# Narrowing the gated layer's weights in 54 smaller steps, at other places of the expert loop

## The chip, the cores and the metric

One core of one Trainium2 chip runs the whole program. The metric is the device time of one execution in microseconds (us), the lower the better. Engines are called TensorE (PE in the profile, its weight loads PEld), VectorE (DVE), ScalarE (ACT), GpSimd (POOL) and SyncE (SP, which only issues transfers here).

## What is computed

Three layers follow one another on 3072 tokens of width 384. The weights of all three come in as 64-bit floats.

```
attention: state = f * state + k v^T;  y = q state        (4 x 8 heads, 768 steps, width 48)
x = y as [3072, 384]
experts:   logits = x @ w_gate; each token goes to one of 8 experts, 384 tokens each, by falling logit
           out[tokens of e] = relu(x @ w1[e]) @ w2[e]     (w1[e]: 384 x 1024, w2[e]: 1024 x 384)
gated:     xn = x / rms(x) * rms_g
           result = (silu(xn @ w_gate) * (xn @ w_val)) @ w_out     (384 x 1536, 384 x 1536, 1536 x 384)
```

## The kernel before

**The stages.** The program runs attention and the routing of the tokens to experts (to about 150 us), the eight experts one after the other (to about 372 us), and the gated layer in twelve chunks of 256 tokens (to the end).

**Matrix products.** Each product of 32-bit floats is made of three matmuls (`mm3`, L620 to L624): both operands are split into a high part and a remainder, and high x high, remainder x high and high x remainder are added up in PSUM. So each operand needs a rounding on ScalarE (the high part) and a subtraction, on VectorE as a rule (the remainder).

**An expert** (`expert`, L1068) is a loop over j = 0 to 7, called slots here. In slot j TensorE makes `h` of block j of 128 hidden columns (nine matmuls of 384 columns), ScalarE takes the relu and rounds it (`hh`, L1082), VectorE makes its remainder (`hl`, L1083), and TensorE multiplies block j - 2 by its piece of w2 (`second`, L979, nine matmuls into `x2`). After slot 7 the `second` of blocks 6 and 7 follow at once, and ScalarE copies `x2` out (`finish`, L975). Each engine works through its instructions in the order of the program.

**Beside it** `side` (L1035) puts in each slot the work for later: in slots 1 to 4 one of the four weight pieces of the next expert is split (`piece_split`, L806: `w`, 1536 columns, ScalarE and then VectorE L813); slots 5 to 7 turn and split the next expert's tokens (`xpose`, L962: three transposes into `xT`, then `xhi` on ScalarE and `xlo` on VectorE L973); slot 0 gathers the tokens of the expert after (`gather`, three indirect transfers on GpSimd); `w_load` issues the loads of pieces on SyncE's queue (L803). In the last expert the pieces of the gated layer take their place (`w2_load`, `piece_split(W2[...])`, two of them on GpSimd).

**Narrowing.** The gated layer's weights are too large to be used as 64-bit floats, and are turned to 32 bits while the experts run, written to DRAM (`w32`) and read from there by `w2_load`. A call of `narrow_step` (L1016) does up to three things, each for another step: it issues the store of a finished step on ScalarE's queue (L1018), works on a step whose load was issued two calls before (`narrow2`, L998), and issues the load of a new one on SyncE's queue (`narrow`, L995). `narrow2` is one multiplication on ScalarE (`nr`, L1004), three integer operations on VectorE (`nb` L1005, `nb` L1006, `ne` L1008) and two on GpSimd (a multiplication L1009 and an addition L1010). A step is 128 x 384 weights; there are 36 of them, and an expert has a call in each of slots 1 to 4, 6 and 7. The first two slots of an expert without a call are 0 and 5.

**The last expert.** In its slot 0 the squares of the first chunk of the gated layer are added up (`n0.squares`, L905: squares on ScalarE, `ss` L911 and the remainder `sl` L915 on VectorE; they lie in `nraw` buffers), and in its slot 2, behind `second`, TensorE sums them over the partitions (`n0.total`, L919 and L920).

**What sets the order** around the change is the program's text alone: `side` is called at the end of a slot's code, and every engine and queue takes its part of it in that order. Buffers of a name rotate; a tile's next use waits for the last reader of its former content.

Of the kernel before, what the change touches and what calls it, by code (L numbers as in the profile page):

```python
# [7 lines left out]
F32 = mybir.dt.float32  # L8
F32R = mybir.dt.float32r
BF = mybir.dt.bfloat16  # L10
I32 = mybir.dt.int32
# [69 lines left out]
class Route:  # L81
# [27 lines left out]
    def range(self, n):  # L109

        nc, v = self.tc.nc, self.v
        m = self.m0[:, 0:n]
        nc.vector.tensor_reduce(out=m, in_=self.lg[:, 0:n], axis=AX.X, op=OP.max)
        nc.vector.tensor_reduce(out=v[:, 1:2], in_=self.lg[:, 0:n].rearrange("p n e -> p (n e)"), axis=AX.X, op=OP.min)
        nc.vector.tensor_reduce(out=v[:, 0:1], in_=m, axis=AX.X, op=OP.max)
        nc.vector.tensor_reduce(out=v[:, 2:3], in_=m, axis=AX.X, op=OP.min)
        nc.vector.tensor_scalar(v[:, 1:3], v[:, 1:3], -1.0, None, op0=OP.mult)
        self.n = n
# [623 lines left out]
def tile_kernel(ctx, tc, q, k, v, f_logit, w_gate, w1, w2, w2_gate, w2_val, w2_out, rms_g, fT, kT, qT, vL, out):  # L742
# [11 lines left out]
    wide = w2_gate.dtype != F32  # L754
# [43 lines left out]
    def piece(pool, rpool, src, shape, eng, hold=False):  # L798

        raw = rpool.tile([128, 1536], F32, name="wraw").rearrange("p (a b) -> p a b", a=shape[0])  # L800
        if hold:
            nc.gpsimd.memset(raw[0:1, 0, 0:1], 0.0)
        nc.sync.dma_start(raw, src)  # L803
        return [pool, raw, shape, eng]

    def piece_split(p, cp=None):  # L806
        pool, raw, shape, eng = p
        hi, lo = (pool.tile([128, 1536], F32R, name="w").rearrange("p (a b) -> p a b", a=shape[0]) for _ in range(2))
        if cp is None:
            nc.scalar.copy(hi, raw)  # L810
        else:
            cp.tensor_scalar(hi, raw, 1.0, 0.0, op0=OP.mult, op1=OP.add)
        eng.tensor_tensor(out=lo, in0=raw, in1=hi.bitcast(F32), op=OP.subtract)  # L813
        p[:] = [(hi, lo)]
# [8 lines left out]
    def w_src(e, i):  # L823
        s = slice((i % 2) * 512, (i % 2) * 512 + 512)
        if i < 2:
            return w1[e, :, s].rearrange("(c p) f -> p c f", p=128), (KD, 512)
        return w2[e, s].rearrange("(c p) f -> p c f", p=128), (4, DM)
# [4 lines left out]
    def gather(e):  # L832
        if e not in XG:
            XG[e] = [xp.tile([128, DM], F32, name="xrow") for _ in range(KD)]
        for c, t in enumerate(XG[e]):
            nc.gpsimd.indirect_dma_start(out=t, out_offset=None, in_=x_dram[:, :],
                                         in_offset=bass.IndirectOffsetOnAxis(
                                             ap=idx[:, 3 * e + c:3 * e + c + 1], axis=0))
# [3 lines left out]
    def w_load(e, i):  # L842
        W1[e, i] = piece(wpool, rawp, *w_src(e, i), nc.vector, e == 1 and i < 2)
# [10 lines left out]
    with ExitStack() as st:  # L854
        with tc.tile_pool(name="rw", bufs=9) as rw, tc.tile_pool(name="rwp", bufs=4, space=PSUM) as rwp:
            rows = Rows(tc, YT, x_dram, ident, rw, rwp)
            rows.put(2)
            rows.take(2)
            R = R[0]
            R.copy()  # L860
            w_load(0, 0)

            def side(s):
                if s < 3:
                    w_load(0, s + 1)
                if 0 < s < 5:
                    pool, raw, shape, _ = W1[0, s - 1]
                    hi, lo = (pool.tile([128, 1536], F32R, name="w").rearrange("p (a b) -> p a b", a=shape[0])
                              for _ in range(2))
                    nc.scalar.copy(hi, raw)  # L870
                    parts[s - 1] = hi, lo, raw

            R.run(5, flag, idx, ident, rows, side)
            gather(0)
# [65 lines left out]
    def prep(c, d, X, eng):  # L940
        s = xn[:, d, c * TC:(c + 1) * TC]
        hi, lo = (t[:, d, 0:TC] for t in X)
        nc.scalar.copy(hi, s)  # L943
        eng.tensor_tensor(out=lo, in0=s, in1=hi.bitcast(F32), op=OP.subtract)  # L944

    W2 = {}
    with ExitStack() as c1:
        P = lambda name, bufs, **kw: c1.enter_context(tc.tile_pool(name=name, bufs=bufs, **kw))
        hp = P("m1h", 3, side="right")
        tp = P("m1t", 1, side="right")  # L950
# [5 lines left out]
        def w2_load(i):  # L956
            if i < 7:
                W2[i] = piece(wpool, rawp, *w2_src(i), nc.gpsimd if i in (1, 3) else nc.vector)
# [3 lines left out]
        def xpose(e, d):  # L962
            if d == 0:
                XT[e] = xt_tiles()
            o = psT.tile([128, CAP], F32, name="xT")
            for c in range(3):
                nc.tensor.transpose(o[:, c * 128:(c + 1) * 128], XG[e][c][:, d * 128:(d + 1) * 128], ident)
            split(e, d, o)
# [13 lines left out]
                mm3(nc, x2[m], [t[:, j % 4, m * 128:(m + 1) * 128] for t in w], H[j], j == 0, j == KF - 1)  # L982

        def nraw():
            return tp.tile([128, 384, 2], I32, name="nraw", bufs=3)

        def narrow(i, h):

            n = 384
            src = w64[i].rearrange("a b -> (a b)").rearrange("(h p c) -> h p c", p=128, c=2 * n)[h]  # L990
            dst = w32[i][:, :].rearrange("a b -> (a b)").rearrange("(h p c) -> h p c", p=128, c=n)[h]
            raw = nraw()
            if len(todo) > 33:
                nc.gpsimd.memset(raw[0:1, 0:1], 0)
            nc.sync.dma_start(raw.rearrange("p c two -> p (c two)"), src)  # L995
            return raw, dst

        def narrow2(raw, dst):  # L998
            n = 384
            hw, lw = raw[:, :, 1], raw[:, :, 0].bitcast(U32)  # L1000
            b = tp.tile([128, n], I32, name="nb", bufs=2)
            e2 = tp.tile([128, n], I32, name="ne")
            r = tp.tile([128, n], F32, name="nr", bufs=3)
            nc.scalar.mul(r, lw, 2.0 ** -52)  # L1004
            nc.vector.tensor_scalar(b, hw, 3, 0x3FFFFFFF, op0=OP.logical_shift_left, op1=OP.bitwise_and)  # L1005
            nc.vector.scalar_tensor_tensor(out=b, in0=hw, scalar=-0x40000000, in1=b, op0=OP.bitwise_and,  # L1006
                                           op1=OP.bitwise_or)
            nc.vector.tensor_scalar(e2, b, -0x800000, None, op0=OP.bitwise_and)  # L1008
            nc.gpsimd.tensor_tensor(out=r, in0=r, in1=e2.bitcast(F32), op=OP.mult)  # L1009
            nc.gpsimd.tensor_tensor(out=r, in0=r, in1=b.bitcast(F32), op=OP.add)  # L1010
            return dst, r

        todo = [(i, h) for i in range(3) for h in range(12)] if wide else []
        ready, done = [], []

        def narrow_step():  # L1016
            if len(done) > 1 or (done and not ready):
                nc.scalar.dma_start(*done.pop(0))  # L1018
            if len(ready) > 1 or (ready and not todo):
                done.append(narrow2(*ready.pop(0)))  # L1020
            if todo:
                ready.append(narrow(*todo.pop(0)))
# [3 lines left out]
        def first_parts():  # L1026
            X0.extend(xt_tiles())
            return [t[:, 0, 0:TC] for t in X0]

        n0 = Norm(0, tp, psT, "xT", lambda n: nraw().rearrange("p c two -> p (c two)").bitcast(F32)[:, :TC], first_parts)  # L1030
        tail0 = n0.steps()[2:]
        NORM0 = {(E - 1, 0): [n0.squares], (E - 1, 2): [n0.total], (E - 1, 3): tail0[0:2], (E - 1, 4): tail0[2:3]}
        del tail0[:3]

        def side(e, j):  # L1035
            if e + 1 < E:
                if j == 0:
                    gather(e + 1)
                    w_load(e + 1, 1)
                if 0 < j < 5:  # L1040
                    narrow_step()
                    piece_split(W1[e + 1, j - 1])
                if j in (1, 2):
                    w_load(e + 1, j + 1)
                if j > 4:
                    xpose(e + 1, j - 5)
                if j == 7:
                    if e + 2 < E:
                        w_load(e + 2, 0)
                    else:  # L1050
                        w2_load(0)
                if j > 5:
                    narrow_step()
            else:
                if j < 6:
                    w2_load(j + 1)
                if j:
                    piece_split(W2[j - 1])
                if j == 5:
                    for f in tail0:  # L1060
                        f()
                if j == 6:
                    for d in range(KD):
                        prep(0, d, X0, nc.gpsimd)
            for f in NORM0.get((e, j), ()):
                f()
# [60 lines left out]
    with ExitStack() as c1:  # L1127
# [35 lines left out]
        for c in range(NCH):  # L1163
            O = [psO.tile([128, DM], F32, name=f"o{m}") for m in range(MB)]
            Hs = {}
            for j in range(KG):
# [10 lines left out]
                h = hp.tile([128, T], F32, name="hf")  # L1177
# [76 lines left out]
```

## Time and profile before

| | |
|---|---|
| time, median of three runs | 832.44 us (831.95 to 832.62) |
| profiled execution | 832.29 us |
| its span, first to last instruction | 830.6 us |
| TensorE: matmuls busy | 805.3 us, 97% of the span |
| TensorE: weight loads busy | 777.4 us, 94% |
| VectorE, ScalarE, GpSimd busy | 485.7, 391.3, 274.0 us |
| mean granted clock of TensorE | 0.985 of full speed; 1.00 in the experts |

The span is the time from the first to the last instruction in the trace; the execution's own time is 1.69 us longer, by what lies around it. Busy matmuls overlap, so that a busy TensorE is not one at its peak. The views read below are the page's busy times, the waits by engine, busy times by stretch, and timelines: a row of a timeline has the start in us from the start of the span, the length, the engine, the line, the operation with its output and inputs, and in brackets how long the engine was idle before it and what ended that. A group of three matmuls may be printed as one row (x3).

### The profile page before, as it was taken

The page shows a single profiled execution, that of the slowest core. Times are in us where ns is not written, and L with a number is a line of the kernel's source. Part 1 is how long each engine was busy: PE and PEld are TensorE (multiplying, and loading weights), DVE is VectorE, ACT ScalarE, POOL GpSimd, SP SyncE. Part 2 cuts the span into 40 slices and gives each one's busy share as a digit, 9 for nine tenths or more (in the row PEclk, how much of TensorE's full clock was granted, in tenths as well). Part 3 has the DMA queues.
Part 4 walks back from the last instruction along what each step waited for, and adds up shares of the span by engine and source line. Part 5 has one row for each costly group of instructions (what it writes and reads, how often), then busy time and mean ns, then how long its engine had stood idle before and what let it go on. Part 6 is the DMA issues. An engine that isn't in the chain of part 4 may idle for free.

```text
span 830.6 us, 16688 instructions
## 1 busy us (share of the span) xinstructions
PE 805.3 (97%) x6641; PEld 777.4 (94%) x6641; DVE 485.7 (58%) x875; ACT 391.3 (47%) x834; POOL 274.0 (33%) x327
## 2 busy tenths in 40 slices
PE   8999996999999999999999999999999999999996
PEld 7888875899999999999999999999999999999996
DVE  8988868579888988575444434334343434334332
ACT  5777644256645555476343343424343443434221
POOL 7877600367777777250202010110102010110100
PEclk9999997899999999999999999999999999999999
DMA  9997227586887788341000000000000000000000
GB/s 270 224 219 193 58 92 290 184 298 226 284 280 245 248 282 301 127 152 39 10 12 20 1 20 2 20 1 20 4 17 20 1 21 1 20 1 21 1 20 20
DMA packets 43829, 88.56 MB, mean 107 GB/s; under 512 B 5440, under 2 KB 23104, under 8 KB 43744
## 3 DMA queue, kind: packets, MB, share of 16 engines
q1 hardware_dynamic: 34672, 70.89, 27.6%
q0 software_dynamic: 3072, 9.44, 3.4%
q10 hardware_dynamic: 6000, 7.09, 2.4%
q8 instruction: 54, 0.88, 0.5%
q14 instruction: 31, 0.25, 0.1%
HBM read 70.89 MB, written 16.52 MB: 105 GB/s over the span
## 4 chain that ended last, share of the span: by engine, by line
PE 61%; issue 9%; DVE 8%; ACT 2%; DMA 1%; POOL 1%; ACTq 0%; DVEq 0%; POOLq 0%
PE o L624 5%; PE o L622 5%; PE o L623 5%; PE g L622 5%; PE g L624 5%; PE g L623 5%; PE v L624 5%; PE v L623 5%; PE v L622 5%; PE x L623 3%; PE x L624 2%; PE x L622 2%; DVE nb L1006 2%; DVE w L813 2%; PE h L623 2%
## 5 line engine op out<-in xcount | busy, mean ns | idle before, releaser
L1178 DVE TENSOR_TENSOR hf<-sg,v 128x256 f32<-128x256 f32 x144 | 60.0, 417 | 165.1 <-PE v L624 114.9
L944 POOL TENSOR_TENSOR xlo<-xn,xhi 128x256 fp32r<-128x256 f32 x36 | 29.5, 823 | 311.9 <-ACT xhi L943 311.9
L1181 ACT CAST hh<-hf 128x256 fp32r<-128x256 f32 x144 | 58.6, 407 | 132.9 <-DVE hf L1178 132.9
L624 PE MATMUL g<-xhi,w 128*128 128x256 f32 x432 | 119.3, 276 | 0.0
L623 PE MATMUL g<-xlo,w 128*128 128x256 f32 x432 | 119.3, 276 | 0.0
L624 PE MATMUL v<-xhi,w 128*128 128x256 f32 x432 | 119.2, 276 | 0.0
L622 PE MATMUL v<-xhi,w 128*128 128x256 f32 x432 | 119.2, 276 | 0.0
L623 PE MATMUL v<-xlo,w 128*128 128x256 f32 x432 | 119.2, 276 | 0.0
L622 PE MATMUL g<-xhi,w 128*128 128x256 f32 x432 | 119.2, 276 | 0.0
L1182 DVE TENSOR_TENSOR hl<-hf,hh 128x256 fp32r<-128x256 f32 x144 | 61.3, 426 | 68.1 <-ACT hh L1181 67.6
L624 PE MATMUL o<-w,hl 128*128 128x384 f32 x288 | 98.6, 342 | 0.0
L622 PE MATMUL o<-w,hh 128*128 128x384 f32 x288 | 97.5, 339 | 0.2 <-ACT hh L1181 0.2
L623 PE MATMUL o<-w,hh 128*128 128x384 f32 x288 | 97.1, 337 | 0.0
L1176 ACT ACTIVATE sg<-g 128x256 f32<-128x256 f32 x144 | 55.3, 384 | 87.8 <-PE g L624 87.3
L622 PEld LDWEIGHTS g<-xhi,w 128*128 128x128 f32 x432 | 81.1, 188 | 0.0
L624 PEld LDWEIGHTS g<-xhi,w 128*128 128x128 f32 x432 | 81.1, 188 | 0.0
L622 PEld LDWEIGHTS v<-xhi,w 128*128 128x128 f32 x432 | 81.1, 188 | 0.0
L624 PEld LDWEIGHTS v<-xhi,w 128*128 128x128 f32 x432 | 81.1, 188 | 0.0
L623 PEld LDWEIGHTS v<-xlo,w 128*128 128x128 f32 x432 | 81.1, 188 | 0.0
L623 PEld LDWEIGHTS g<-xlo,w 128*128 128x128 f32 x432 | 81.0, 188 | 0.0
L1009 POOL TENSOR_TENSOR nr<-nr,ne 128x384 f32<-128x384 f32 x36 | 61.6, 1711 | 42.8 <-ACT hh L1082 11.8
L623 PE MATMUL x<-hl,w 128*128 128x384 f32 x192 | 65.7, 342 | 3.5 <-DVE hl L1083 3.5
(237 smaller groups left out, 1893.8 us busy)
## 6 DMA issues: line engine op xcount, KB each, us to landing
wraw<-in_moe_w_dram SPq DMA_DIRECT2D x32, 768.0 KB, 7.8
v<-in_v_rows_dram SPq DMA_DIRECT2D x16, 288.0 KB, 5.1
x_dram<-xrows SPq DMA_DIRECT2D x24, 192.0 KB, 5.4
nraw<-in_moe_w_gate_dram SPq DMA_DIRECT2D x12, 384.0 KB, 4.9
nraw<-in_moe_w_val_dram SPq DMA_DIRECT2D x12, 384.0 KB, 4.4
nraw<-in_moe_w_out_dram SPq DMA_DIRECT2D x12, 384.0 KB, 4.3
raw_f<-in_f_logit_turned_dram SPq DMA_DIRECT2D x26, 144.0 KB, 5.4
raw_k<-in_k_turned_dram SPq DMA_DIRECT2D x26, 144.0 KB, 4.6
```

The costliest lines, as they stand in the source:

```text
L622: nc.tensor.matmul(out, lhs[0], rhs[0], start=first, stop=False)
L623: nc.tensor.matmul(out, lhs[0], rhs[1], start=False, stop=False)
L624: nc.tensor.matmul(out, lhs[1], rhs[0], start=False, stop=last)
L813: eng.tensor_tensor(out=lo, in0=raw, in1=hi.bitcast(F32), op=OP.subtract)
L944: eng.tensor_tensor(out=lo, in0=s, in1=hi.bitcast(F32), op=OP.subtract)
L1006: nc.vector.scalar_tensor_tensor(out=b, in0=hw, scalar=-0x40000000, in1=b, op0=OP.bitwise_and, op1=OP.bitwise_or)
L1009: nc.gpsimd.tensor_tensor(out=r, in0=r, in1=e2.bitcast(F32), op=OP.mult)
L1176: nc.scalar.activation(sg, pg, AF.Silu)
L1178: nc.vector.tensor_tensor(out=h, in0=sg, in1=pv, op=OP.mult)
L1181: nc.scalar.copy(hh, h)
L1182: nc.vector.tensor_tensor(out=hl, in0=h, in1=hh.bitcast(F32), op=OP.subtract)
```

## The change

A step becomes 128 x 256 weights, so that there are 54. Calls of `narrow_step` are taken out of slots 1 to 4. Slots 5, 6 and 7 of each expert but the last now have two calls, and so has slot 0 of experts 1 to 6; in the last expert slots 0, 1 and 2 have two each, in which the last two steps are worked on and the last stores issued. A step waits one call longer for its store. The buffers are more and smaller: `nraw` four, `nb` three, `ne` two and `nr` five in place of three, two, one and three, which is 18,432 bytes of a partition before and after. Before the first four loads (three before) GpSimd touches the buffer.

```diff
--- before.py
+++ after.py
@@ -982,25 +982,25 @@
                 mm3(nc, x2[m], [t[:, j % 4, m * 128:(m + 1) * 128] for t in w], H[j], j == 0, j == KF - 1)
 
         def nraw():
-            return tp.tile([128, 384, 2], I32, name="nraw", bufs=3)
+            return tp.tile([128, 256, 2], I32, name="nraw", bufs=4)
 
         def narrow(i, h):
 
-            n = 384
+            n = 256
             src = w64[i].rearrange("a b -> (a b)").rearrange("(h p c) -> h p c", p=128, c=2 * n)[h]
             dst = w32[i][:, :].rearrange("a b -> (a b)").rearrange("(h p c) -> h p c", p=128, c=n)[h]
             raw = nraw()
-            if len(todo) > 33:
+            if len(todo) > 49:
                 nc.gpsimd.memset(raw[0:1, 0:1], 0)
             nc.sync.dma_start(raw.rearrange("p c two -> p (c two)"), src)
             return raw, dst
 
         def narrow2(raw, dst):
-            n = 384
+            n = 256
             hw, lw = raw[:, :, 1], raw[:, :, 0].bitcast(U32)
-            b = tp.tile([128, n], I32, name="nb", bufs=2)
-            e2 = tp.tile([128, n], I32, name="ne")
-            r = tp.tile([128, n], F32, name="nr", bufs=3)
+            b = tp.tile([128, n], I32, name="nb", bufs=3)
+            e2 = tp.tile([128, n], I32, name="ne", bufs=2)
+            r = tp.tile([128, n], F32, name="nr", bufs=5)
             nc.scalar.mul(r, lw, 2.0 ** -52)
             nc.vector.tensor_scalar(b, hw, 3, 0x3FFFFFFF, op0=OP.logical_shift_left, op1=OP.bitwise_and)
             nc.vector.scalar_tensor_tensor(out=b, in0=hw, scalar=-0x40000000, in1=b, op0=OP.bitwise_and,
@@ -1010,11 +1010,11 @@
             nc.gpsimd.tensor_tensor(out=r, in0=r, in1=b.bitcast(F32), op=OP.add)
             return dst, r
 
-        todo = [(i, h) for i in range(3) for h in range(12)] if wide else []
+        todo = [(i, h) for i in range(3) for h in range(18)] if wide else []
         ready, done = [], []
 
         def narrow_step():
-            if len(done) > 1 or (done and not ready):
+            if len(done) > 2 or (done and not ready):
                 nc.scalar.dma_start(*done.pop(0))
             if len(ready) > 1 or (ready and not todo):
                 done.append(narrow2(*ready.pop(0)))
@@ -1037,8 +1037,10 @@
                 if j == 0:
                     gather(e + 1)
                     w_load(e + 1, 1)
+                if e and not j:
+                    narrow_step()
+                    narrow_step()
                 if 0 < j < 5:
-                    narrow_step()
                     piece_split(W1[e + 1, j - 1])
                 if j in (1, 2):
                     w_load(e + 1, j + 1)
@@ -1049,9 +1051,13 @@
                         w_load(e + 2, 0)
                     else:
                         w2_load(0)
-                if j > 5:
+                if j > 4:
+                    narrow_step()
                     narrow_step()
             else:
+                if j < 3:
+                    narrow_step()
+                    narrow_step()
                 if j < 6:
                     w2_load(j + 1)
                 if j:
```

VectorE in an expert of the middle, before: slots 0 and 1 (the two `hl` at the top) and the start of slot 2. The names are those above; `x2` merges two like rows.

```order
L1083 SCALAR_TENSOR_TENSOR hl<-h,hh 128x384 x2
L1005 TENSOR_SCALAR nb<-nraw 128x384
L1006 SCALAR_TENSOR_TENSOR nb<-nraw,nb 128x384
L1008 TENSOR_SCALAR ne<-nb 128x384
L813 TENSOR_TENSOR w<-wraw,w 128x1536
L1083 SCALAR_TENSOR_TENSOR hl<-h,hh 128x384
L1005 TENSOR_SCALAR nb<-nraw 128x384
```

Slot 1 is a step and a piece, and slots 2 to 4 repeat it. Slots 5 to 7, before:

```order
L1083 SCALAR_TENSOR_TENSOR hl<-h,hh 128x384
L973 TENSOR_TENSOR xlo<-xT,xhi 128x384
L1083 SCALAR_TENSOR_TENSOR hl<-h,hh 128x384
L973 TENSOR_TENSOR xlo<-xT,xhi 128x384
L1005 TENSOR_SCALAR nb<-nraw 128x384
L1006 SCALAR_TENSOR_TENSOR nb<-nraw,nb 128x384
L1008 TENSOR_SCALAR ne<-nb 128x384
L1083 SCALAR_TENSOR_TENSOR hl<-h,hh 128x384
L973 TENSOR_TENSOR xlo<-xT,xhi 128x384
```

Here slot 5 has no step, and slots 6 and 7 have one each. VectorE at the end of slot 4, in slots 5 and 6 and at the start of slot 7 with the change (lines of `expert` are six higher there):

```order
L813 TENSOR_TENSOR w<-wraw,w 128x1536
L1089 SCALAR_TENSOR_TENSOR hl<-h,hh 128x384
L973 TENSOR_TENSOR xlo<-xT,xhi 128x384
L1005 TENSOR_SCALAR nb<-nraw 128x256
L1006 SCALAR_TENSOR_TENSOR nb<-nraw,nb 128x256
L1008 TENSOR_SCALAR ne<-nb 128x256
L1005 TENSOR_SCALAR nb<-nraw 128x256
L1006 SCALAR_TENSOR_TENSOR nb<-nraw,nb 128x256
L1008 TENSOR_SCALAR ne<-nb 128x256
L1089 SCALAR_TENSOR_TENSOR hl<-h,hh 128x384
L973 TENSOR_TENSOR xlo<-xT,xhi 128x384
L1005 TENSOR_SCALAR nb<-nraw 128x256
L1006 SCALAR_TENSOR_TENSOR nb<-nraw,nb 128x256
```

Between two `hl` of slots 1 to 4 there was a step and a piece, and is now a piece alone; between the `hl` of slots 5, 6 and 7 and the one behind each there were no, one and one step, and are now two.

VectorE in slot 0 of the last expert, with the change; before, the rows from L1005 to L1008 were not there:

```order
L1089 SCALAR_TENSOR_TENSOR hl<-h,hh 128x384
L1005 TENSOR_SCALAR nb<-nraw 128x256
L1006 SCALAR_TENSOR_TENSOR nb<-nraw,nb 128x256
L1008 TENSOR_SCALAR ne<-nb 128x256
L1005 TENSOR_SCALAR nb<-nraw 128x256
L1006 SCALAR_TENSOR_TENSOR nb<-nraw,nb 128x256
L1008 TENSOR_SCALAR ne<-nb 128x256
L911 TENSOR_TENSOR nraw<-nraw 128x256 x2
L915 TENSOR_TENSOR xlo<-nraw,xhi 128x256
```

The two steps stand ahead of the squares that `n0.total` sums.

## Rows read from the trace of the kernel before

**Rows 1.** One expert each: length, then PE, PEld, DVE, ACT, POOL busy us, clock, DMA.

```profile
233.85:261.48 27.63, 26.87 (x155) 26.16 (x153) 24.27 (x34) 14.77 (x24) 20.91 (x15) 1.00 0.80 264
316.69:343.11 26.42, 26.42 (x154) 26.31 (x153) 20.62 (x28) 13.40 (x21) 15.46 (x11) 1.00 0.85 295
```

**Rows 2.** Waits, weight loads of TensorE (whole span): total us, times, longest.

```profile
PEld x L623 <- DVE hl L1083: 6.2, 9, 1.1
```

**Rows 3.** Timeline of one expert, weight loads of TensorE: start, us, [idle before].

```profile
255.47 0.19 PEld L623 LDWEIGHTS x<-hl,w 128*128 128x128 f32 x1 [0.29 <-DVE hl L1083]
259.98 0.19 PEld L623 LDWEIGHTS x<-hl,w 128*128 128x128 f32 x1 [1.07 <-DVE hl L1083]
```

**Rows 4.** The same expert, VectorE: `hl` of slot 5, then slots 6 and 7.

```profile
259.37 0.55 DVE L1083 SCALAR_TENSOR_TENSOR hl<-h,hh 128x384 fp32r<-128x384 f32 x1
261.23 0.39 DVE L1005 TENSOR_SCALAR nb<-nraw 128x384 int32<-128x384 int32 x1
261.66 0.56 DVE L1006 SCALAR_TENSOR_TENSOR nb<-nraw,nb 128x384 int32<-128x384 int32 x1
262.32 0.36 DVE L1008 TENSOR_SCALAR ne<-nb 128x384 int32<-128x384 int32 x1
262.60 0.55 DVE L1083 SCALAR_TENSOR_TENSOR hl<-h,hh 128x384 fp32r<-128x384 f32 x1
263.53 0.52 DVE L1005 TENSOR_SCALAR nb<-nraw 128x384 int32<-128x384 int32 x1
264.08 1.26 DVE L1006 SCALAR_TENSOR_TENSOR nb<-nraw,nb 128x384 int32<-128x384 int32 x1
```

**Rows 5.** The same expert, GpSimd beside them.

```profile
260.39 1.02 POOL L1010 TENSOR_TENSOR nr<-nr,nb 128x384 f32<-128x384 f32 x1
262.82 1.01 POOL L1009 TENSOR_TENSOR nr<-nr,ne 128x384 f32<-128x384 f32 x1 [1.41 <-ACT xhi L972]
263.91 1.02 POOL L1010 TENSOR_TENSOR nr<-nr,nb 128x384 f32<-128x384 f32 x1
```

**Rows 6.** GpSimd and VectorE in expert 1, slot 1.

```profile
188.70 1.02 POOL L1009 TENSOR_TENSOR nr<-nr,ne 128x384 f32<-128x384 f32 x1 [0.37 <-issue]
189.79 2.42 POOL L1010 TENSOR_TENSOR nr<-nr,nb 128x384 f32<-128x384 f32 x1
...
188.82 2.51 DVE L813 TENSOR_TENSOR w<-wraw,w 128x1536 fp32r<-128x1536 f32 x1 [0.26 <-issue]
```

**Rows 7.** Operations of 256 columns: GpSimd (min/median/max ns), VectorE (page, mean ns).

```profile
L944 POOL TENSOR_TENSOR xlo<-xn,xhi x36: 733/737/2288, 366.6 to 782.2; 128x256 fp32r<-128x256 f32 x36
...
L1182 DVE TENSOR_TENSOR hl<-hf,hh 128x256 fp32r<-128x256 f32 x144 | 61.3, 426 | 68.1 <-ACT hh L1181 67.6
```

**Rows 8.** Timeline of expert 6, where TensorE waits for nothing.

```profile
336.10 0.49 PE L967 MATMUL xT<-ident,xrow 128*128 128x128 f32 x3
343.11 0.49 PE L967 MATMUL xT<-ident,xrow 128*128 128x128 f32 x3
345.21 0.34 PE L623 MATMUL x<-hl,w 128*128 128x384 f32 x1
...
344.15 0.56 DVE L973 TENSOR_TENSOR xlo<-xT,xhi 128x384 fp32r<-128x384 f32 x1 [1.34 <-ACT xhi L972]
```

**Rows 9.** Expert 7: VectorE in slot 0, TensorE at the end of slot 2.

```profile
348.93 0.56 DVE L1083 SCALAR_TENSOR_TENSOR hl<-h,hh 128x384 fp32r<-128x384 f32 x1 [4.23 <-ACT hh L1082]
349.54 0.95 DVE L911 TENSOR_TENSOR nraw<-nraw 128x256 f32<-128x256 f32 x2
350.97 0.42 DVE L915 TENSOR_TENSOR xlo<-nraw,xhi 128x256 fp32r<-128x256 f32 x1 [0.47 <-ACT xhi L914]
...
353.10 0.28 PE L920 MATMUL xT<-xlo,onesr 128*128 128x256 f32 x1
```

**Rows 10.** The page, DMA issues: KB each, median us to landing.

```profile
wraw<-in_moe_w_dram SPq DMA_DIRECT2D x32, 768.0 KB, 7.8
nraw<-in_moe_w_gate_dram SPq DMA_DIRECT2D x12, 384.0 KB, 4.9
```

## The prediction

> **What bounds the kernel now.** TensorE, nearly everywhere: its matmuls are busy for 97% of the span (the table). So the change can give back only what TensorE waits for in the experts, where the steps are, or add to it. I read the waits of TensorE's weight loads first: those for `hl` are 6.2 us in nine times [rows 2], and no other wait of theirs falls in the experts' loop. Then two stretches, each from the last transposes of one expert to those of the next: 27.63 us where there are such waits, with the matmuls busy for 26.87; 26.42 us, all busy, where there are none [rows 1]. In the first a short and a long wait (0.29 and 1.07 us, in slots 6 and 7) cost 1.21 [rows 1, 3], so about 0.08 less than each lasts. Nine waits then cost 6.2 - 9 x 0.08 = **5.5 us**: experts 1 to 5, in each the long one, in four the short one too. Expert 6, which has only two steps left, has none.
>
> The timeline of VectorE tells why. In slots 1 to 4 it has a step, a piece and `hl`, more than a slot of TensorE lasts (about 3.2 us, 3.5 with transposes: the transposes of slots 5 and 7 are 7.01 us apart [rows 8]). So `hl` of slot 5 ends at 259.92 [rows 4], and the weight load that waits for it starts at 259.98 [rows 3].
>
> **Two rules read from the rows.** (1) VectorE's operations on SBUF and GpSimd's exclude each other. Alone, a step runs 261.23 to 262.60, 1.37 us; the next one's first `nb` ends 0.22 after GpSimd's multiplication, its second (1.26 for 0.56) 0.41 after the addition [rows 4, 5]. (2) When GpSimd has a second operation queued behind its first, a waiting VectorE goes in between: `w` waited until 189.72, ran to 191.33, and the addition due at 189.79 ended at 192.21 [rows 6]. `hl` and `xlo` read PSUM and keep 0.55 beside GpSimd.
>
> At 256 columns GpSimd's operations take 0.73 us, not 1.02 [rows 5, 7]. For VectorE, 0.426 at 256 against 0.55 at 384 [rows 7, 8] is 0.13 per 128 columns, half that where an operation goes at double pace (`ne`, 0.36): 0.29, 0.43 and 0.29, with gaps 1.1 us for a step alone. The tail behind a wait shrinks likewise, to 0.15 and 0.28.
>
> **The change, part by part.** *Slots 1 to 4 lose their steps.* VectorE needs there 0.47 for `hl` (start to start) and 1.7 for `w`, 2.2 of 3.2 us, so it catches up about 1 us a slot. The nine waits go: **-5.5 us**. What is late next stands in slot 7.
>
> *Slots 5 and 6 get two steps each.* The tightest is now `hl` of slot 7, since the two `second` behind slot 7 follow at once. Let X be the start of `xlo` in slot 5. It follows its transposes by 344.15 - 343.11 = 1.04; without waits X = 336.10 + 1.04 = 337.14 [rows 8]. From X, by the durations and rules:
>
> - First step 0.46 to 1.60. GpSimd multiplies 1.74 to 2.47.
> - Second step: first `nb` to 1.80; the second waits for the multiplication, ends 2.75; the addition runs to 3.34; `ne` waits for it, ends 3.49. The pair took 2.94.
> - `hl` 3.40, `xlo` 3.87, third step from 4.33: its second `nb` waits for the addition of the second step (to 5.20), ends 5.48; `ne` 5.88.
> - Fourth: second `nb` waits for a multiplication (to 6.75), 7.03; `ne` for an addition (to 7.62), 7.77. Pair: 3.35.
> - `hl` of slot 7 ends at 8.23.
>
> That is 345.37. The matmul that reads it started at 345.21 [rows 8], its weight load 0.18 earlier, 345.03; with 0.06 from `hl` to load it comes **0.40 late**, for 0.32. Experts 1 to 6 have this (in expert 0 the first pair falls in slot 6, behind nothing): **+1.9 us**. The bounds: two pairs of unhindered steps (2.2 each) leave 1.4 us to spare, no cost; two at the length of a hindered step of 384 (263.53 to 265.8, 2.3) would be 9.2, 3.3 late. I take the worked value, since its durations have rows at 256; between the hindered step scaled by two thirds (1.5, 6.1 the two pairs, 0.2 late) and mine it hardly moves.
>
> Whether `ne` waits for GpSimd has no row: in the kernel before it never met a GpSimd operation on data. I take it as the first `nb`, which has its duration and does wait.
> The Trainium skill (SBUF — State Buffer, Who interferes with whom) speaks for it: tensor_scalar can enter a mode that takes the port pair shared with GpSimd, and the other engine then blocks until the end. By that page the sum stays as here; rule (1) agrees with it where [rows 4 to 6] show it.
>
> *Slot 0 gets two, slot 7 one more*: `hl` of slots 0 and 1 are used two slots later, 3 us or more to spare. No cost.
>
> *Expert 7, slot 0*, is the one place where two steps go ahead of something short of time. There `ss` starts 0.61 behind the start of `hl` and `sl` ends 1.85 later, at 351.39; TensorE reads it at 353.10 [rows 9], so the load has 1.5 to spare. GpSimd still works on the steps of slot 7, so the pair takes 3.4 us more between `hl` and `ss` by the same rules, and `ss` and `sl` (two SBUF operands) each wait out one of its operations, 0.3 in all. With everything 0.32 later: 351.39 + 0.32 + 3.44 + 0.31 = 355.46, the load at 355.52 where TensorE would have come at 353.24: 2.3 late, **+2.2 us**. Bounds: 0.5 for unhindered pairs, 3.6 if all wait once more.
>
> *Other engines and queues, at nothing.* ScalarE has 18 more `nr` and stores, but is busy for 14.8 of 27.6 us [rows 1]. A store waits for its addition, in front of the next `nr`; the third step's, due 0.6 before `hl` of slot 7 ends, holds nothing until the copies of `x2`. GpSimd has 16 x 0.73 = 11.7 us of it per expert for 12 x 1.02. On SyncE a load of 256 KB follows the second `nb` four steps back, 8 us ahead of its use; 384 KB landed in 4.9 [rows 10]. The last two pieces of weights now queue behind loads that wait for slot 7's steps, about 3.5 us after `hl` of slot 7; at 7.8 to landing [rows 10] the first comes some 1.7 after its slot could use it, within the 4 us that slots 1 to 4 have gained. If that cover goes, X moves.
>
> **Sum.** -5.5 + 1.9 + 2.2 = -1.4 us: 832.29 - 1.4 = 830.9 for the profiled execution; the median lay 0.15 above it: **831.0 us**. A measurement of this kernel tells about 0.2%, 1.7 us, from no change, so this is just inside.
>
> **The rivals.** *Faster: no new wait at slot 7.* If `ne` doesn't wait, each pair is 0.34 shorter, `hl` of slot 7 0.3 early, and the last expert costs 1.5: -5.5 + 1.5 = -4.0, 828.4 us. For it: 0.4 us is all that is missing. Against: the first `nb` waits. 0.25.
>
> *Slower: GpSimd's addition goes ahead of the waiting VectorE.* Each `nb` then sits out both operations; the pairs grow by 0.93 together, `hl` of slot 7 is 1.33 late, 1.25 x 6 = 7.5, and expert 7 costs 3.6: -5.5 + 11.1 = +5.6, 838.0 us. It decides from two pairs of 6.5 us on (mine: 6.3), where 6 x 0.55 + 2.2 eats the gain. Against it [rows 6]; for it, that one row of another operation carries the rule. 0.17.
>
> *The change doesn't do what it says:* the old waits stay, because late transfers or `w` hold slots 1 to 4. Then 1.9 + 2.2 = +4.1, 836.5 us. Against: expert 6 keeps the four pieces, has two steps and no wait. 0.08.
>
> **Numbers.** My forecast has 0.5, and with its bounds reaches from 829 to 833: of it 0.17 lies below 830.8. With the first rival faster has 0.42, slower 0.23 (the second and third, nearly whole), the same 0.35. The range takes in the first rival and the third, and leaves the second's worst out: 827.8 to 836.5.
>
> **What would show it.** In the new profile: weight loads waiting for `hl` in slots 6 and 7 on blocks 4 and 5 gone; about six waits of 0.4 us for `hl` of slot 7; one of 2.3 us for the remainder of the squares in expert 7; second `nb` and `ne` of about 0.9 and 0.6 us beside GpSimd. No wait for `hl` at all, or over 1 us of it per expert, would make the forecast wrong, and so would a wait for a weight piece.

## The result: 0.6% slower, and the profile after

The changed kernel takes **838.24 us** (median of 5 runs, 835.88 to 838.97) against 831.95 us (5 runs, 831.38 to 832.62): ratio 1.0059, 95% interval 1.0043 to 1.0075. Its profiled execution has a span of 836.5 us at a mean clock of 0.982; before it was 830.6 us at 0.985.

Where the difference lies is read from four marks on TensorE: the last transposes of expert 0, those of expert 6, the matmul of L919 (the sum of the squares in expert 7) and the end.

| us | before | after | difference | predicted |
|---|---|---|---|---|
| start to expert 0's last transposes | 179.34 | 178.80 | -0.5 | 0 |
| from there to expert 6's (six experts) | 163.77 | 166.18 | **+2.4** | -3.9 |
| from there to L919 | 9.87 | 12.11 | +2.2 | +2.5 |
| from there to the end | 477.62 | 479.41 | +1.8 | 0 |
| sum | | | +5.9 | -1.4 |

The wait for `hl` of slot 7 comes behind the last transposes of its expert, so of the six waits that the prediction adds (0.32 us each) five belong to the second row and expert 6's to the third. The first stage varies by some microseconds between runs whatever the kernel (178 to 182 us in the runs below), so stages are compared from expert 0's last transposes on.

The stretches that end with the last transposes of experts 1, 2 and 5, in the view of busy times by stretch (columns as in [rows 1]), answer to [rows 1]:

```profile
178.80:207.19 28.39, 27.18 (x154) 26.10 (x153) 19.37 (x33) 13.77 (x24) 15.63 (x19) 1.00 0.69 238
207.19:238.04 30.85, 28.05 (x154) 27.36 (x153) 25.84 (x46) 16.36 (x28) 20.57 (x22) 0.94 0.70 240
...
291.38:318.18 26.80, 26.69 (x155) 26.25 (x154) 24.17 (x40) 15.23 (x26) 20.60 (x19) 1.00 0.75 257
```

The later experts are 0.8 us shorter than the disturbed ones of before (27.63), and 0.38 over the bare 26.42: so for them the forecast holds. The first two stretches take 1.6 and 4.05 us more than 26.80, and the second has a clock of 0.94. The waits of TensorE's weight loads from 178 us on (columns as in [rows 2]) answer to [rows 2]:

```profile
PEld x L623 <- DVE hl L1089: 6.6, 8, 2.8
PEld xT L919 <- ACT xhi L914: 2.0, 1, 2.0
...
PEld xT L920 <- DVE xlo L915: 0.3, 1, 0.3
```

The nine old waits have become eight others with as much time in them, one of 2.8 us, and the wait for the squares has come.

**The steady experts are as worked out.** This is the timeline around the two pairs of one expert, VectorE with GpSimd's first two operations and the weight load at the end. It answers to [rows 4, 5] and to the estimate of 8.23 us from `xlo` of slot 5 to the end of `hl` of slot 7:

```profile
312.20 0.56 DVE L973 TENSOR_TENSOR xlo<-xT,xhi 128x384 fp32r<-128x384 f32 x1 [1.35 <-ACT xhi L972]
...
313.53 0.29 DVE L1008 TENSOR_SCALAR ne<-nb 128x256 int32<-128x256 int32 x1
...
314.06 0.92 DVE L1006 SCALAR_TENSOR_TENSOR nb<-nraw,nb 128x256 int32<-128x256 int32 x1
315.08 0.64 DVE L1008 TENSOR_SCALAR ne<-nb 128x256 int32<-128x256 int32 x1
...
319.95 0.55 DVE L1089 SCALAR_TENSOR_TENSOR hl<-h,hh 128x384 fp32r<-128x384 f32 x1
...
313.95 0.74 POOL L1009 TENSOR_TENSOR nr<-nr,ne 128x256 f32<-128x256 f32 x1 [2.30 <-ACT hh L1088]
314.77 0.80 POOL L1010 TENSOR_TENSOR nr<-nr,nb 128x256 f32<-128x256 f32 x1
...
320.55 0.19 PEld L623 LDWEIGHTS x<-hl,w 128*128 128x128 f32 x1 [0.44 <-DVE hl L1089]
```

From 312.20 to 319.95 + 0.55 = 320.50 are 8.30 us. `ne` does wait for GpSimd (0.64 for 0.29). The waiting `nb` gets in ahead of the addition queued at 314.77: it ends at 314.98, 0.29 behind the multiplication (313.95 + 0.74 = 314.69), and the addition at 315.57. The load waits 0.44.

**The start-up is not.** First a row of GpSimd in the kernel before, then timelines of the changed kernel from the end of expert 0 through expert 1, GpSimd and SyncE's queue first, then ScalarE, VectorE, TensorE:

```profile
159.72 0.12 POOL L994 MEMSET nraw<- 1x2 int32 x2
...
179.62 0.24 POOL L994 MEMSET nraw<- 1x2 int32 x1
181.47 0.09 POOL L994 MEMSET nraw<- 1x2 int32 x1
...
179.89 2.03 SPq L995 DMA_DIRECT2D nraw<-in_moe_w_gate_dram  x2
...
184.31 3.69 SPq L995 DMA_DIRECT2D nraw<-in_moe_w_gate_dram  x2
189.38 0.95 SPq L803 DMA_DIRECT2D wraw<-in_moe_w_dram  x2
...
182.66 0.45 ACT L1004 ACTIVATE nr<-nraw 128x256 f32<-128x256 uint32 x1 [2.85 <-DMA nraw<-in_moe_w_gate_dram]
...
198.40 1.48 ACT L810 CAST w<-wraw 128x1536 fp32r<-128x1536 f32 x1 [3.44 <-DMA wraw<-in_moe_w_dram]
...
211.88 0.55 DVE L1089 SCALAR_TENSOR_TENSOR hl<-h,hh 128x384 fp32r<-128x384 f32 x1
...
212.48 0.69 PE L623 MATMUL x<-hl,w 128*128 128x384 f32 x1 [2.45 <-DVE hl L1089]
```

Ahead of the prediction it is said that the kernel before touches three `nraw` buffers. It touches two (its `len(todo) > 33` is asked when one of the 36 steps has already been taken out). Both touches run at 159.72, before any step is on GpSimd. The touches of the third and fourth buffer are new, and in the changed kernel (L994) they are written at calls 3 and 4, in slot 6 of expert 0. There they stand on GpSimd behind the multiplications and additions of the first two steps, so the loads of steps 3 and 4 cannot start before these touches end, at 179.86 and 181.56. ScalarE stands 2.85 us for the first of the two loads, the narrowing slips, and the next loads of SyncE stand at its head for their buffers. The third and fourth weight piece of the next expert come behind them, at 189.38, and are cast from 198.40 on. So `w` and two pairs of steps are pressed together ahead of `hl` of slot 7 (211.88), and TensorE stands 2.45 us for it. That is expert 1's last `hl`; it comes behind the last transposes, so it lies in the second stretch. The first stretch has shorter waits from the same delay: 0.72 us for an `hh` that the held ScalarE makes late, and 0.98 us for the `hl` behind the third piece's `w`.

**Expert 7**, the timeline of VectorE and TensorE; it answers to [rows 9]:

```profile
351.18 0.56 DVE L1089 SCALAR_TENSOR_TENSOR hl<-h,hh 128x384 fp32r<-128x384 f32 x1
...
355.33 1.27 DVE L911 TENSOR_TENSOR nraw<-nraw 128x256 f32<-128x256 f32 x2
357.07 0.42 DVE L915 TENSOR_TENSOR xlo<-nraw,xhi 128x256 fp32r<-128x256 f32 x1 [0.47 <-ACT xhi L914]
...
357.09 0.38 PE L919 MATMUL xT<-xhi,onesr 128*128 128x256 f32 x1 [1.70 <-ACT xhi L914]
```

`ss` (printed `nraw`) starts 4.15 us behind `hl`, before 0.61: TensorE waits 1.70 us for its high part and 0.3 more for its remainder. What the clock did behind this wait and behind that of 2.45 us stands in the busy times of 2 us each (granted clock in the third column from the right):

```profile
210.00:212.00 2.00, 0.03 (x1) 0.00 (x0) 1.86 (x5) 0.30 (x1) 1.51 (x2) 1.00 1.06 398
212.00:214.00 2.00, 1.52 (x5) 1.52 (x6) 1.93 (x4) 0.92 (x2) 1.51 (x2) 0.53 0.72 253
214.00:216.00 2.00, 2.00 (x9) 2.00 (x8) 1.79 (x4) 0.97 (x3) 1.42 (x2) 0.61 1.05 399
216.00:218.00 2.00, 2.00 (x14) 2.00 (x13) 0.59 (x2) 0.86 (x2) 1.57 (x3) 1.00 0.90 292
...
358.00:360.00 2.00, 2.00 (x10) 2.00 (x9) 1.01 (x2) 2.00 (x3) 0.00 (x0) 0.73 0.40 132
360.00:362.00 2.00, 2.00 (x8) 2.00 (x8) 1.24 (x2) 1.98 (x2) 1.20 (x1) 0.50 0.09 15
362.00:364.00 2.00, 2.00 (x12) 2.00 (x11) 0.56 (x1) 1.99 (x4) 2.00 (x1) 0.92 0.96 316
```

Twice the clock falls to its half level (1.2 for 2.4 GHz) once TensorE works again. Behind L919 the three rows lose 2 x (0.27 + 0.50 + 0.08) = 1.7 us of full speed, nearly all of the last stage's +1.8. Behind the wait of 2.45 us it is 1.52 x 0.47 + 2 x 0.39 = 1.5 us.

### The profile page after: what moved, and what is told of

The parts are those of the page before. It is cut to its first block, busy times and chain, and to the rows that moved or that the text cites. A ratio compares the mean times of both kernels' runs of the same rounds, so it can differ in the third digit from the quotient of the medians.

```text
span 836.5 us, 16925 instructions
## 1 busy us (share of the span) xinstructions
PE 808.6 (97%) x6641; PEld 779.8 (93%) x6641; DVE 494.0 (59%) x929; ACT 395.7 (47%) x852; POOL 274.7 (33%) x365
## 4 chain that ended last, share of the span: by engine, by line
PE 64%; issue 8%; DVE 5%; DMA 2%; ACT 2%; POOL 1%; DVEq 0%; POOLq 0%; ACTq 0%
PE o L624 5%; PE o L622 5%; PE o L623 5%; PE g L622 5%; PE g L623 5%; PE g L624 5%; PE v L624 5%; PE v L623 5%; PE v L622 5%; PE h L623 3%; PE x L623 3%; PE h L622 3%; PE h L624 3%; PE x L624 3%; PE x L622 3%
## 5 line engine op out<-in xcount | busy, mean ns | idle before, releaser
L1009 POOL TENSOR_TENSOR nr<-nr,ne 128x256 f32<-128x256 f32 x54 | 52.6, 974 | 61.6 <-ACT hh L1088 36.2
L813 DVE TENSOR_TENSOR w<-wraw,w 128x1536 fp32r<-128x1536 f32 x35 | 64.7, 1849 | 12.9 <-ACT w L810 11.8
```

## The experiments

Theory A is the reading above: gain and steady price as forecast, and on top of them the touches at the start and the clock behind the waits. The expectations name the theories against it. Ratios are to runs of the kernel before on the same chip.

**e1: touches ahead of the steps.** The four buffers are taken and touched in slot 5 of expert 0, before any step is on GpSimd.

```diff
-            raw = nraw()
-            if len(todo) > 49:
-                nc.gpsimd.memset(raw[0:1, 0:1], 0)
+            raw = held.pop(0) if held else nraw()
...
+            if e == 0 and j == 5:
+                for _ in range(4):
+                    held.append(nraw())
+                    nc.gpsimd.memset(held[-1][0:1, 0:1], 0)
```

> The changed kernel with one edit: GpSimd touches the four nraw buffers at the start of slot 5 of expert 0, ahead of the first step, so that the loads of the third and fourth step no longer wait behind the first two steps on GpSimd. Theory A (these two loads start late, ScalarE waits for them in slot 7, and everything behind, the loads of weight pieces too, slips): no wait for a load of nraw in expert 0, experts 1 and 2 take 26.8 us each like experts 4 to 6 (28.4 and 30.9 in the changed kernel), no fall of the clock near 212 us, time about 832. Theory B (the transfers are too many at once, 128 x 512 words in rows of 2 KB, and late wherever they start): experts 1 and 2 keep over 28 us, time 837 to 839.

834.23 us, ratio 1.0009 (0.9993 to 1.0024). SyncE issues all four loads by 166.3 us. In its profile the first two stretches take 26.19 and 26.78 us where they took 28.39 and 30.85, and the six experts 159.70 for 166.18; the prediction's terms for this stretch give 163.77 - 5.5 + 5 x 0.32 = 159.9. The third and fourth weight piece are issued 5.0 us behind expert 0's last transposes (183.54 - 178.50; after: 10.6) and the third cast starts at 11.9 (after: 19.6). SyncE's four loads, and the waits from 178 us on:

```profile
163.66 2.65 SPq L993 DMA_DIRECT2D nraw<-in_moe_w_gate_dram  x4
...
PEld x L623 <- DVE hl L1091: 2.8, 6, 0.6
PEld xT L919 <- ACT xhi L914: 2.0, 1, 2.0
```

What is left is the forecast's own pattern: six waits for `hl` of slot 7 and the one for the squares. Theory A holds in the profile and B falls: the place of four touches cost 6.5 us there. The median lies 2.2 us above A's 832, which is taken up at the end ("Still open").

**e2: squares ahead of the steps** in expert 7, the squares in `nb` buffers.

```diff
-        NORM0 = {(E - 1, 0): [n0.squares], (E - 1, 2): [n0.total], ...
+        NORM0 = {(E - 1, 2): [n0.total], ...
...
+                if j == 0:
+                    n0.squares()
                 if j < 3:
                     narrow_step()
```

> The changed kernel with the squares of the first chunk put ahead of the two steps in slot 0 of expert 7 (their two short-lived tiles are nb buffers there). Theory A (the two steps delay the remainder sl, TensorE waits 1.7 to 2 us, and its clock falls after that wait): the wait at L919 and L920 goes, the granted clock from 357 to 380 us is 1.00 and not 0.94, together 4 us: about 834. Theory C (the fall of the clock there has another cause, such as the busier VectorE and transfers): only the wait of 2.2 us goes, 836, and the clock stays at 0.94.

838.88 us, ratio 1.0059 (1.0041 to 1.0077): a miss. Theory C's 836 is missed too. The wait at L919 and the fall of the clock behind it are gone, but from expert 6's last transposes to the end it is 491.03 us for 491.52, -0.5 and not -4. The waits of that stretch show why; `hl` is late instead:

```profile
PEld x L623 <- DVE hl L1092: 3.9, 6, 1.3
```

The longest, 1.27 us, is for expert 6's last `hl`, where a weight piece came late (a cast on ScalarE waits 1.79 us for its load). The other five, 2.6 us together, are in expert 7, behind the two steps that are worked on in its slot 0.

**e3: e1 and e2 together.**

> Both edits in one kernel. Theory A: the two add up, 10 us under the changed kernel, 828; left are the waits for hl of slot 7, about 0.4 us in each of experts 1 to 6, which is some 3 us faster than the kernel before. Theory B: 834 to 836.

831.72 us, ratio 0.9987 (0.9973 to 1.0001): theory A's 828 and B's 834 are both missed. From expert 0's transposes to the end it is 649.94 us, before 651.26. By medians it is 7.2 us under e2, from which it differs in the touches alone.

**e4: e3, and in experts 1 to 6 the second step of slot 6 goes to slot 1.**

```diff
+                if e and j == 1:
+                    narrow_step()
                 if 0 < j < 5:
...
                     narrow_step()
-                    narrow_step()
+                    if not (e and j == 6):
+                        narrow_step()
```

> Both edits, and in experts 1 to 6 one of the two steps of slot 6 moved to slot 1. Theory A (hl of slot 7 is late because two pairs of steps stand ahead of it, each held by GpSimd's operations): the six waits of 0.4 us go, experts take 26.4 us, 2.3 us under the kernel with both edits: about 826. Theory D (those waits are the price of GpSimd's work beside slots 5 to 7 wherever its steps stand): the same as with both edits within 0.5 us.

831.17 us, ratio 0.9976 (0.9959 to 0.9993). The time is 0.55 us under e3's, near D's outcome and far from A's 826. The profile tells them apart: the waits for `hl` of slot 7 are gone and an expert takes 26.42 us, so it was the two pairs in a row (A, not D). But behind L919 it takes 479.81 us, 2.2 more than before. Timelines of GpSimd and ScalarE in expert 7:

```profile
351.10 0.80 POOL L1008 TENSOR_TENSOR nr<-nr,nb 128x256 f32<-128x256 f32 x1
...
351.93 0.33 ACTq L1016 DMA_DIRECT2D w_o<-nr  x1
352.30 1.48 ACT L810 CAST w<-wraw 128x1536 fp32r<-128x1536 f32 x1 [2.27 <-DMA wraw<-w_v]
```

The bracket names a load, but the cast stands on ScalarE behind a store, and the store starts when the addition ends (351.10 + 0.80). A store of the last steps holds up the gated layer's first pieces, and five of TensorE's weight loads in that expert wait 0.3 to 0.7 us for `hl`, 2.3 us together.

**e5: all 54 steps done by expert 6.** The touches move to slot 2 of expert 0; one number per slot says how many calls it has; in expert 7 only stores are left, and the squares are as in the change.

```diff
-                if e and not j:
-                    narrow_step()
-                    narrow_step()
...
-                if j > 4:
-                    narrow_step()
+                for _ in range((2, 1, 0, 0, 0, 2, 1, 2)[j] if e else (0, 0, 1, 1, 1, 2, 1, 2)[j]):
                     narrow_step()
             else:
                 if j < 3:
                     narrow_step()
-                    narrow_step()
```

> The changed kernel with the four touches first, two more calls in expert 0 (slots 2 to 7 hold 1, 1, 1, 2, 1, 2), one step of slot 6 moved to slot 1 in experts 1 to 6, and so no step worked on in expert 7, only the last three stores in slots 0 to 2. Theory A (what is left of the loss after the edits so far is the two steps in expert 7, whose store and split ScalarE and VectorE then do late): no wait of TensorE for hl anywhere in the experts, 26.4 us per expert, and from the sum of squares to the end 477.6 us as in the kernel before (479.8 with two steps there): 646.4 us from the last transposes of expert 0 to the end, 4.9 us under the kernel before, 0.6%. Theory E (the 2.2 us at the end are not the two steps but the smaller stores or the order of the pieces): 479 to 480 stays, 2.7 us under the kernel before.

**827.77 us** (826.41 to 829.14, 5 runs), before 833.07 (20 runs): ratio 0.9943 (0.9928 to 0.9957), faster than both kernels; A holds and E falls. From expert 0's transposes to the end 645.97 us. One wait for `hl` is left, and a steady expert has none:

```profile
PEld x L623 <- DVE hl L1086: 0.5, 1, 0.5
...
284.39:310.81 26.42, 26.42 (x155) 26.31 (x153) 23.83 (x39) 15.25 (x26) 18.11 (x19) 1.00 0.76 256
```

**e8: e5, but two steps in slot 6 and none in slot 1**: the numbers `(2, 0, 0, 0, 0, 2, 2, 2)`, in expert 0 `(0, 0, 0, 1, 1, 2, 2, 2)`, the touches in its slot 3.

> As the one before, but with two steps in slots 0, 5, 6 and 7 of experts 1 to 6 as in the changed kernel (expert 0: one call each in slots 3 and 4 and two in 5 to 7). Theory A: the same but for the wait for hl of slot 7, 0.4 us in each of six experts: 26.8 us each, 2.3 us behind the kernel before this one. Theory D: no difference between the two beyond 0.5 us.

831.01 us, ratio 0.9976 (0.9964 to 0.9989). The waits for `hl` of slot 7 are back, in all seven experts, 5.5 us together (the six experts take 162.30 us, 3.7 more than e5). The direction is theory A's, the size larger. Five of ScalarE's casts wait 1.1 to 2.0 us for a weight piece, but in e5 six wait 1.0 to 2.8 us, so that alone does not explain it; the cause of the larger size is open.

**e6: one step in every slot** of experts 0 to 6, touches in slot 0 of expert 0.

> 54 steps of 256 columns with one call in each of the eight slots of experts 0 to 6, the four touches in slot 0 of expert 0, nothing worked on in expert 7. Theory A (a slot is late only if its steps, its piece and GpSimd's operations together outlast the slack): slots 1 to 4 overrun by 0.5 to 0.9 us each instead of 1.3, 2 to 3.6 us by slot 5, which is under the 4.3 us that the kernel before could bear, so no wait for hl: 26.4 us per expert, 4.5 to 5 us under the kernel before. Theory F (steps beside a piece cost TensorE whatever their size): waits for hl in slots 6 and 7 as in the kernel before, 27 us and more per expert.

841.11 us, ratio 1.0098 (1.0081 to 1.0114): a miss for A, F's outcome, and the slowest of all. Waits, the stretch of one expert, and GpSimd and VectorE in a slot with a step and a piece:

```profile
PEld x L623 <- DVE hl L1086: 15.1, 23, 0.9
...
264.88:293.56 28.68, 27.23 (x155) 25.75 (x154) 24.86 (x39) 15.36 (x26) 20.58 (x19) 1.00 0.70 242
...
308.05 0.75 POOL L1007 TENSOR_TENSOR nr<-nr,ne 128x256 f32<-128x256 f32 x1 [0.82 <-issue]
308.87 2.13 POOL L1008 TENSOR_TENSOR nr<-nr,nb 128x256 f32<-128x256 f32 x1
...
307.83 0.55 DVE L1086 SCALAR_TENSOR_TENSOR hl<-h,hh 128x384 fp32r<-128x384 f32 x1
308.29 2.11 DVE L813 TENSOR_TENSOR w<-wraw,w 128x1536 fp32r<-128x1536 f32 x1
310.33 0.82 DVE L1003 TENSOR_SCALAR nb<-nraw 128x256 int32<-128x256 int32 x1
...
311.93 0.55 DVE L1086 SCALAR_TENSOR_TENSOR hl<-h,hh 128x384 fp32r<-128x384 f32 x1
```

`w` waits for the multiplication (2.11 for 1.76) and the first `nb` for the addition (0.82 for 0.29). From `hl` to `hl` are 4.10 us, where a slot of TensorE lasts about 3.2. So a step in each of the four slots with a piece is too much. One such slot can bear a step: e4 and e5 have one in slot 1.

**e7: the old size at new places.** The kernel before, with 384 columns and its buffers, and the calls of an expert as `(1, 0, 0, 0, 0, 2, 1, 2)`.

```diff
                 if 0 < j < 5:
-                    narrow_step()
                     piece_split(W1[e + 1, j - 1])
...
-                if j > 5:
+                for _ in range((1, 0, 0, 0, 0, 2, 1, 2)[j]):
                     narrow_step()
```

> The kernel before with its 36 steps of 384 columns and its buffers, only the calls moved: none in slots 1 to 4, and 1, 2, 1, 2 in slots 0, 5, 6, 7 of experts 0 to 6. Theory A (the gain is in the places, not in the size): no wait for hl in slots 6 and 7, the two pairs ahead of hl of slot 7 are 5.9 us where 6.1 can be borne: 26.4 us per expert, about 5 us under the kernel before. Theory G (the larger steps hold VectorE and GpSimd longer, so the size is needed): a wait for hl of slot 7 of 0.5 us or more per expert, no more than 2 us under the kernel before.

833.88 us, ratio 1.0010 (1.0000 to 1.0019): a miss for theory A's 5 us. Its waits, and the second step of slot 5 on VectorE:

```profile
PEld x L623 <- DVE hl L1082: 5.9, 5, 1.6
PEld xT L967 <- DMA xrow<-x_dram,idx: 2.4, 2, 2.0
...
284.88 1.27 DVE L1006 SCALAR_TENSOR_TENSOR nb<-nraw,nb 128x384 int32<-128x384 int32 x1
286.25 0.98 DVE L1008 TENSOR_SCALAR ne<-nb 128x384 int32<-128x384 int32 x1
```

Beside GpSimd's longer operations a pair of the old size takes 3.99 us up to the next `hl` (283.17 to 287.16), one of 256 columns 2.96 (312.68 to 315.64 with the change). So theory G's outcome is there: at the new places the old step has its waits at slot 7 instead. Two things are not told apart: the old buffers, fewer of each kind, stayed as well, and 2.4 us of its waits are for a late gather, whose cause is open.

**e9, e10 (the kernel of e1) and e11 (the change) once more**, to see whether the clock falls each time.

> The kernel with the four touches first once more, for a second profile: its first one was 4 us faster than the median of its other executions, and showed the wait of 1.7 us at the sum of squares in expert 7 without a fall of the clock behind it. Theory H (whether the clock falls behind that wait differs from one execution to the next, and costs 1.7 us when it does): a fall to about 0.5 for 3 to 4 us behind the wait in this profile or the next, and the stretch from the last transposes of expert 6 to the end 492 us where it falls and 490.5 where it does not. Theory I (something else is slower in the other executions): no fall, and the time is lost elsewhere, ahead of the experts or in them.

> The same kernel a third time. Theories as for the run before.

> The changed kernel once more, for a second profile. Theory A: the same waits as in its first profile, for the loads of the third and fourth step in slot 7 of expert 0 (2 to 3 us), for hl of slot 7 in expert 1 (2 to 2.5 us) and at the sum of squares in expert 7 (1.7 to 2 us), since order and buffers set them; the clock falls behind the one in expert 1, and may or may not behind the one in expert 7.

One execution each: 829.84, 831.17 and 840.37 us. Behind the same wait at L919 the clock stays at 1.00 in e9 and falls in e10. First the row of e9, then two of e10:

```profile
350.00:354.00 4.00, 3.92 (x23) 3.73 (x24) 2.99 (x4) 3.92 (x5) 0.45 (x1) 1.00 0.30 99
```

```profile
350.00:354.00 4.00, 3.91 (x14) 3.71 (x15) 3.02 (x4) 3.92 (x5) 0.39 (x2) 0.63 0.30 99
354.00:358.00 4.00, 4.00 (x24) 4.00 (x23) 1.50 (x3) 3.99 (x6) 3.22 (x1) 0.95 0.58 199
```

From expert 6's transposes to the end it is 490.42 us in e9 and 491.60 in e10: the fall costs 1.2 us there. e11 has the waits of the change again, 2.4 us for expert 1's last `hl` and 1.7 at L919, with a fall behind both. So theory H holds: the fall differs between executions.

## Why the prediction was wrong

It said 831.0 us, from 827.8 to 836.5; 838.24 lies outside.

**The failed step is "Other engines and queues, at nothing".** Two of its sentences fell together. "On SyncE a load of 256 KB follows the second `nb` four steps back" is true from the fifth step on; the first four follow a touch on GpSimd, two of which stand there behind steps. And "within the 4 us that slots 1 to 4 have gained" was the cover of the last two weight pieces: it was worked out for an expert in its stride, while expert 1 starts with the narrowing already late, so that the third cast is 7.7 us later than in e1. The text said "if that cover goes, X moves", and gave it no price. e1 gives it: 166.18 - 159.70 = 6.5 us, of it some 1.5 by the clock. With the touches moved the rest of the sum comes out: from expert 0's transposes to the end e1 takes 1.1 us and e9 1.6 us less than the kernel before, where -1.4 was forecast; e10, in which the clock falls behind L919, takes 0.2 more.

**A second term was missing: what a wait does to the clock.** The wait of 1.70 us at L919 drew 1.7 more behind it. e1, e9 and e10 show that this falls in some executions and not in others.

**Nine old waits, -5.5: right.** e5 has them gone and nothing in their place: 651.26 - 645.97 = 5.3 us in the profiles.

**Slot 7, +1.9: right.** 0.44 for 0.40 us late, 0.38 for 0.32 an expert, and e4 takes it away by parting the two pairs. In six experts that saves 0.6 us against e3 (158.95 for 159.58) and not 5 x 0.38, because three of e3's stretches have the wait and still take 26.47 to 26.63 us: for some 96 matmuls in a row in each, they start 0.173 us apart and not 0.177, at the same granted clock of 1.00. Why they do so is open. That `ne` waits was chosen without a row; it does, and so the faster rival falls. The 0.64 us measured agree with what the prediction takes from the Trainium skill (SBUF — State Buffer, Who interferes with whom).

**Expert 7, +2.2: right in size** (12.11 - 9.87 = 2.24, of which 0.38 is expert 6's slot 7, so 1.9 for 2.2), though TensorE waits mainly for the high part of the squares and not for their remainder. It is not a cost of its order alone: e2 shows that the other order swaps it for 2.6 us of waits for `hl` in that expert. The two steps have no room there; e5 takes them out.

**The rivals.** The slower one gave 838.0 us, near the time measured, but for another reason: GpSimd's addition did not go ahead of the waiting VectorE (314.06 and 314.77 above). "The old waits stay, because late transfers or `w` hold slots 1 to 4" came nearest: late transfers did, but at the start only.

**Still open.** e1's ten runs have a median of 834.2 us where its profiled executions took 830.4, 829.8 and 831.2. Most of that goes with the clock: in the 33 runs of the kernel before that stand beside e1, the time falls by 0.48 us for each 0.001 of mean clock (least squares over their list), in e1's by 0.51, and e1's median clock is 0.9845 where the profiled execution had 0.990: 5.5 x 0.51 = 2.8 of 3.9 us. In which stage the other runs lost it was not seen, since they have no trace. Nor does the mean clock tell: it takes in the stretch from 130 to 155 us, mostly ahead of the experts, where the granted clock is 0.66 in the traces of before and after, 0.73 in e1 and 0.80 in e5.

## What to carry to other kernels

A plan that is right in its stride can lose all of it at the start: follow every gate of the first few steps (a touch, a free buffer, the head of a queue) through the program order of each engine, and ask what waits behind it in the same queue. Here small steps did best where VectorE has no long operation, or once beside one, and not as two pairs in a row ahead of a tile that is wanted soon; that with all of them done before the last expert gave 0.6% (e5). A wait of about 2 us on TensorE may cost nearly as much again by the clock, so it is worth more than its length.

## What was not expected of the hardware

Behind waits of 1.70 and 2.45 us the granted clock of TensorE fell from 1.00 to about half for 3 to 4 us, and lost 1.2 to 1.7 us each time; after the same wait in another execution of the same kernel it stayed at 1.00 (e9, e10). The Trainium skill (TensorE: Matmul & The Clock Gate, Part 1) says that the gate looks at the engine at times of its own, which are not tied to the program, and that the same kernel so differs from run to run; e9 and e10 agree. Over all timed executions the kernels with one of these two waits have median clocks of 0.984 and 0.9845 (the change, e1, e2), the others 0.987 to 0.989 (e3 to e8). It is a tendency and no rule: e7 has a wait of 2.0 us for a gather and 0.989, and the runs of the kernel before, which has neither wait, reach from 0.984 to 0.992.
